# Transposed 32x32 blocks go from SBUF to SBUF in four transfers, without a DRAM tile

## The chip, the core and the metric

The kernel runs on one core of a Trainium2 chip. The metric is the device time of one execution in microseconds; less is better. The core has the engines PE (matmuls), DVE, ACT and POOL (elementwise), and the queue of SP, which here issues nearly all transfers between DRAM and SBUF.

## What is computed

A chunked attention over 4 batches, 8 heads, 768 positions and 64 features, and then a two-layer network on its output. Each chunk of 32 queries sees 16 positions to the left, its own 32, 8 to the right, and 8 memory positions: 64 keys.

```python
for c in range(nc):                      # 24 chunks of 32
    k_full = np.concatenate([mem_k, k[:, :, l_start:r_end]], axis=2)
    v_full = np.concatenate([mem_v, v[:, :, l_start:r_end]], axis=2)
    scores = scale * np.matmul(q_c, k_full.transpose(0, 1, 3, 2))
    scores = scores - np.max(scores, axis=-1, keepdims=True)
    a = np.exp(scores)
    a = a / (np.sum(a, axis=-1, keepdims=True) + 1e-09)
    out[:, :, c_start:c_end] = np.matmul(a, v_full)
...
h = x @ w_in                             # x: 3072 x 512, w_in: 512 x 2048
P = a[0] + a[1] * h + a[2] * h2 + a[3] * h3
Q = 1.0 + np.abs(b[0]) * np.abs(h) + np.abs(b[1]) * h2
return (P / (Q + 1e-06)) @ w_out         # w_out: 2048 x 512
```

## The kernel before

The 3072 tokens are 8 blocks of 384 (`TB`), half a batch each. The network runs in rounds: round n takes a block i and one of 16 slices j of the inner 2048. `g1` (L386, 12 matmuls) makes h for the slice, a chain of elementwise steps on ACT, DVE and POOL (L442 to L480) makes g as a high and a low part (`ghi`, L473, and `glo`, L480, both on POOL), and `g2` (L401, 9 matmuls) adds g times w_out into the three PSUM tiles `o` of the block. `order` sets the rounds: slices 0 to 9 of blocks 0 and 1, all of block 2, slices 10 to 15 of block 1, then of block 0, then blocks 3 to 7. The sums of the first ten slices of blocks 0 and 1 are kept in DRAM (`part`); `fetch` loads them into the tiles `stage` ahead of the block's end, and `evac` (L425, DVE) adds them to `o`.

The input of a block, `x_hi` and `x_lo`, comes from its attention, which runs in pieces between the rounds, for 4 pairs of heads p per block (a unit is one (i, p)). For blocks 3 to 7 (`BLOCKWISE` = 3) the pieces of a unit are:
- `att_scores` (b, PE L277), `att_max` (m, DVE: max and subtraction L293 into `e`, written with the two heads side by side), `att_exp` (x, ACT);
- `att_turn` (c): DVE transposes `e` in 32x32 blocks into a tile `blocks` (`turn_blocks`, L301); then `across` moves the blocks to their places in `eT`;
- `att_values` (d, PE L328): `eT` times v;
- `att_norm` (n, DVE): the row sums' inverse (L336, L337), and the scaling L339 into `xt`;
- `att_back` (e): `xt` is transposed in the same way and goes through `across` into `xf`;
- `att_hi` (h, ACT L353) copies `xf` into `x_hi`, `att_lo` (l, POOL L364) makes `x_lo`.

`across` writes `blocks` with one transfer into a DRAM tile and reads it back with four, one for each group of 32 destination partitions. The four reads wait for the write to have landed. There are two `blocks` tiles, two `eT` and two `xf` tiles, each in turn.

Every instruction and transfer keeps the order of the program on its engine (`pin`, and `load`, which issues on SP's queue, L117). SP issues in order: a transfer that waits holds up all those behind it. In the queue stand, mixed with those of `across`, the loads of q, k and v of later units, the `stage` loads and the stores of the output. The rounds up to 29 are in an order written out by hand (`SEQ`); from 30 on (`HAND`) a plan places the pieces: `attend(n, "db")` ahead of g1, and `attend(n, "xhlencmQ")` at the end of the round.

Of the kernel before, what the change touches and what calls it, by code (L numbers as in the profile page):

```python
# [12 lines left out]
F32 = mybir.dt.float32  # L13
# [3 lines left out]
ALU = mybir.AluOpType  # L17
AX = mybir.AxisListType

CHUNK = 32  # L20
# [12 lines left out]
BLOCKWISE = 3  # L33
# [32 lines left out]
def attn_moe(ctx, tc, qk, vm, w, a, b, out):  # L66
    nc = tc.nc
    P = 128
    NBLK, NPAIR = qk.shape[:2]
    NJT, DM = w.shape[0], out.shape[1]  # L70
    D = DM // (2 * NPAIR)
    TB = out.shape[0] // NBLK
    NC = TB // CHUNK
    NG = TB // P
    KEYS = P // 2
# [9 lines left out]
    dr = ctx.enter_context(tc.tile_pool(name="dr", bufs=1, space=bass.MemoryType.DRAM))  # L85
# [26 lines left out]
    def pin(ins):  # L112
        if pinned[0]:
            tc.keep_in_program_order(ins)

    def load(dst, src, queue=nc.sync):
        ins = queue.dma_start(out=dst, in_=src)  # L117
        if in_order[0]:
            tc.keep_in_program_order(ins)
# [139 lines left out]
        return [(g, j, 4 * g + j if i < BLOCKWISE else NG * j + g) for g in range(NG) for j in range(4)]  # L259

    def across(blocks, name):
        kept = dr.tile([P, TB], F32, name=name, tag=name, bufs=2)
        load(kept, blocks)
        t = at.tile([P, TB], F32, name=name, tag=name, bufs=XB.get(name, 1))
        n = TB // 4
        for b in range(4):
            load(t[b * CHUNK:(b + 1) * CHUNK].rearrange("k (j n) -> k j n", n=n),
                 kept.rearrange("(j k) (b n) -> b k j n", k=CHUNK, n=n)[b])
        return t

    def att_scores(i, p):
# [8 lines left out]
    def att_max(i, p):  # L280
        u = unit[i, p]
        s = u.pop("s")
        sv = s[:, :NG * 2 * KEYS].rearrange("x (g h w) -> x g h w", g=NG, h=2)
        if i % 2 == 0:
            pin(nc.vector.memset(sv[0:CHUNK, 0, :, 0:LEFT], NEG))
        else:
            pin(nc.vector.memset(sv[P - CHUNK:P, NG - 1, :, WIN - RIGHT:WIN], NEG))
        mx = sm.tile([P, NG * 2], F32, name="mx")
        s3 = s[:, :NG * 2 * KEYS].rearrange("x (n w) -> x n w", w=KEYS)
        pin(nc.vector.tensor_reduce(mx, s3, axis=AX.X, op=ALU.max))  # L290
        e = u["e"] = at.tile([P, NG, KEYS, 2], F32, name="e", tag="e", bufs=2)
        top = mx.rearrange("x (g h) -> x g h", g=NG).unsqueeze(3).broadcast_to([P, NG, 2, KEYS])
        pin(nc.vector.tensor_tensor(e.rearrange("x g w h -> x g h w"), sv, top, op=ALU.subtract))  # L293

    def att_exp(i, p):
        e = unit[i, p]["e"]
# [7 lines left out]
    def att_turn(i, p):  # L304
        u = unit[i, p]
        if i >= BLOCKWISE:
            u["eT"] = across(turn_blocks(u.pop("e").rearrange("x g w h -> x g (w h)")), "eT")
            return
        ep = u["ep"] = pa(i)
        e = u.pop("e")  # L310
        for g in range(NG):
            pin(nc.tensor.transpose(out=ep[:, g * P:(g + 1) * P], in_=e[:, g], identity=ident))
# [19 lines left out]
    def att_norm(i, p):  # L332
        u = unit[i, p]
        on = u.pop("o")[:, :NG * 2 * (D + 1)].rearrange("x (n d) -> x n d", d=D + 1)
        rinv = sm.tile([P, NG * 2], F32, name="rinv")
        pin(nc.vector.tensor_scalar(rinv.unsqueeze(2), on[:, :, D:D + 1], 1e-9, W_SCALE, op0=ALU.add, op1=ALU.mult))  # L336
        pin(nc.vector.reciprocal(rinv, rinv))  # L337
        xt = u["xt"] = at.tile([P, NG * 2, D], F32, name="xt", tag="xt")
        pin(nc.vector.tensor_tensor(xt, on[:, :, :D], rinv.unsqueeze(2).broadcast_to([P, NG * 2, D]), op=ALU.mult))  # L339

    def att_back(i, p):
        u = unit[i, p]
        if i >= BLOCKWISE:
            u["xp"] = across(turn_blocks(u.pop("xt").rearrange("x (g h) d -> x g (h d)", h=2)), "xf")
            return
        xp = u["xp"] = pa(i)
        xt = u.pop("xt")
        for g in range(NG):
            pin(nc.tensor.transpose(out=xp[:, g * P:(g + 1) * P], in_=xt[:, 2 * g:2 * g + 2, :], identity=ident))
# [54 lines left out]
    kept = []  # L404
# [88 lines left out]

    att = {}
    pieces = dict(b=att_scores, m=att_max, x=att_exp, c=att_turn, k=att_keep, d=att_values, n=att_norm, e=att_back, h=att_hi, l=att_lo)

    def plan(n, kind, i, p):
# [135 lines left out]
def windows(x, mem):  # L633
    B, H, S, D = x.shape
    n = S // CHUNK
    rows = np.arange(n)[:, None] * CHUNK + np.arange(WIN)
    x = np.pad(x, ((0, 0), (0, 0), (LEFT, RIGHT), (0, 0)))[:, :, rows]
    mem = np.broadcast_to(mem[:, :, None], (B, H, n) + mem.shape[2:])
    return np.concatenate([x, mem], axis=3)


def lay_out(q, k, v, mem_k, mem_v):
    B, H, S, D = q.shape
    n = S // CHUNK // 2
    kw, vw = windows(k, mem_k), windows(v, mem_v)
    keys = kw.shape[3]
    kt = kw.reshape(B, H // 2, 2, 2, n * keys, D).transpose(0, 3, 1, 2, 5, 4).reshape(2 * B, H // 2, 2, D, n * keys)
    qt = q.reshape(B, H // 2, 2, 2, n * CHUNK, D).transpose(0, 3, 1, 2, 5, 4).reshape(2 * B, H // 2, 2, D, n * CHUNK)
    qk = np.stack([np.concatenate([kt[:, :, 0], qt[:, :, 0]], axis=3),
                   np.concatenate([qt[:, :, 1], kt[:, :, 1]], axis=3)], axis=2)  # L650
    vw = np.concatenate([vw, np.ones(vw.shape[:4] + (1,), vw.dtype)], axis=4)
    vm = vw.reshape(B, H // 2, 2, 2, n, keys, D + 1).transpose(0, 3, 1, 2, 5, 4, 6)
    return qk, np.ascontiguousarray(vm.reshape(2 * B, H // 2, 2, keys, n * (D + 1)))


# [16 lines left out]
```

## Time and profile before

| | |
|---|---|
| median of 3 runs | 651.05 us (650.72 to 652.34) |
| profiled execution | 647.67 us |
| its span | 645.9 us |
| PE busy | 615.8 us (95%) |
| DVE busy | 494.4 us (77%) |
| ACT busy | 432.7 us (67%) |
| POOL busy | 431.2 us (67%) |
| mean granted clock of PE | 0.984 |

The span goes from the first to the last instruction of the profiled execution; the rest of its time lies around it. Busy time is a share of the whole span; the stretches differ, and the rows below are read by stretch. The granted clock is 1.00 at 2.4 GHz and 0.50 at 1.2 GHz. In a timeline the last part in brackets is the time in which the engine had nothing to do before the instruction, and what released it.

### The profile page before, as it was taken

The numbers are of one execution on the slowest core, as the hardware profiler recorded it, in microseconds if no ns is written. First come the engines' busy times: TensorE is split into PE (matmuls) and PEld (weight loads), VectorE is DVE, ScalarE is ACT, GpSimd is POOL, SyncE is SP. The second block draws the span as 40 slices with busy tenths as digits, with TensorE's granted clock in tenths as the row PEclk, the third lists the DMA queues.
The fourth block names the chain that finished last, engine by engine and source line by source line (L and its number), as shares of the span: only waits on it lengthen the run. The fifth ranks groups of instructions, "written<-read, shape, count | busy, mean of one in ns | idle before, by whom it ended". The sixth has DMA issues, their size and how long they took to land.

```text
span 645.9 us, 12289 instructions
## 1 busy us (share of the span) xinstructions
PE 615.8 (95%) x4312; PEld 536.7 (83%) x4312; DVE 494.4 (77%) x961; ACT 432.7 (67%) x814; POOL 431.2 (67%) x457
## 2 busy tenths in 40 slices
PE   4779999999999999799999999999999999999997
PEld 3477787889988888698988888889888888999995
DVE  5878998997967887778777777877777777766665
ACT  4667878778856666466666766676666766676664
POOL 5557776977966657556666666676766666776662
PEclk8879999999999999899999999999999999999999
DMA  7998136304122555554333532234333310000001
GB/s 251 380 381 303 43 91 238 114 1 154 52 92 81 166 185 159 162 160 154 114 103 105 157 114 86 76 99 144 103 99 112 119 55 25 24 28 23 2 1 49
DMA packets 49326, 77.55 MB, mean 120 GB/s; under 512 B 27121, under 2 KB 32241, under 8 KB 48881
## 3 DMA queue, kind: packets, MB, share of 16 engines
q1 hardware_dynamic: 48016, 72.04, 34.4%
q10 hardware_dynamic: 960, 3.16, 1.5%
q0 software_dynamic: 288, 1.57, 0.7%
q8 instruction: 34, 0.56, 0.4%
q14 instruction: 28, 0.22, 0.1%
HBM read 59.44 MB, written 17.30 MB: 119 GB/s over the span
## 4 chain that ended last, share of the span: by engine, by line
issue 23%; PE 21%; POOL 20%; DVE 13%; DMA 12%; SPq 5%; ACT 5%; POOLq 0%; DVEq 0%; ACTq 0%
PE h L386 10%; PE o L401 8%; POOL glo L480 8%; POOL ghi L473 7%; SPq L117 5%; DMA xf<-blocks 3%; POOL cy L447 2%; DMA qk<-in_qk_dram 2%; DVE ct L466 2%; POOL x_lo L364 2%; DMA eT<-blocks 2%; DMA w_raw<-in_w_dram 2%; DVE cr L467 2%; DMA v_main<-in_vm_dram 2%; DVE stage L170 2%
## 5 line engine op out<-in xcount | busy, mean ns | idle before, releaser
L386 PE MATMUL h<-x_hi,w_hl 128*128 128x384 f32 x1024 | 268.1, 343 | 3.3 <-DVE ct L457 3.2
L401 PE MATMUL o<-w_hl,ghi 128*128 128x512 f32 x768 | 241.4, 395 | 4.2 <-POOL ghi L473 3.2
L447 POOL TENSOR_TENSOR cy<-cy,ha 128x384 f32<-128x384 f32 x128 | 130.1, 1016 | 145.5 <-ACT cy L443 140.8
L386 PEld LDWEIGHTS h<-x_hi,w_hl 128*128 128x128 f32 x1024 | 186.7, 190 | 17.2 <-issue 5.4
L386 PE MATMUL h<-x_lo,w_hl 128*128 128x384 f32 x512 | 173.7, 339 | 0.0
L401 PEld LDWEIGHTS o<-w_hl,ghi 128*128 128x128 f32 x768 | 141.9, 189 | 26.7 <-POOL ghi L473 3.6
L401 PE MATMUL o<-w_hl,glo 128*128 128x512 f32 x384 | 152.5, 397 | 0.9 <-POOL glo L480 0.6
L480 POOL TENSOR_TENSOR glo<-ct,ghi 128x384 fp32r<-128x384 f32 x126 | 127.8, 1014 | 9.1
L442 ACT ACTIVATE ha<-h 128x384 f32<-128x384 f32 x128 | 62.8, 491 | 97.1 <-PE h L386 92.4
L456 DVE TENSOR_TENSOR ct<-ct,h 128x384 f32<-128x384 f32 x128 | 70.3, 549 | 71.4 <-ACT ct L452 71.2
L473 POOL TENSOR_TENSOR ghi<-ct,zero 128x384 fp32r<-128x384 f32 x126 | 104.3, 828 | 11.2 <-DVE ct L468 8.7
L466 DVE SCALAR_TENSOR_TENSOR ct<-ct,par,cr 128x384 f32<-128x384 f32 x128 | 78.5, 613 | 37.4 <-ACT cr L462 34.9
L461 ACT ACTIVATE cr<-cy 128x384 f32<-128x384 f32 x128 | 63.3, 494 | 58.5 <-POOL cy L447 52.2
L386 PEld LDWEIGHTS h<-x_lo,w_hl 128*128 128x128 f32 x512 | 97.2, 190 | 0.0
L443 ACT ACTIVATE cy<-ha,bab 128x384 f32<-128x384 f32 x128 | 90.9, 710 | 4.3
L401 PEld LDWEIGHTS o<-w_hl,glo 128*128 128x128 f32 x384 | 72.4, 189 | 22.4 <-POOL glo L480 2.7
L452 ACT ACTIVATE ct<-h,par 128x384 f32<-128x384 f32 x128 | 83.9, 656 | 0.0
L457 DVE SCALAR_TENSOR_TENSOR ct<-ct,par,h 128x384 f32<-128x384 f32 x128 | 78.7, 615 | 4.5
L468 DVE SCALAR_TENSOR_TENSOR ct<-cr,ct 128x384 f32<-128x384 f32 x128 | 71.4, 558 | 4.4
L467 DVE SCALAR_TENSOR_TENSOR cr<-cy,cr 128x384 f32<-128x384 f32 x128 | 71.2, 556 | 0.4
L462 ACT ACTIVATE cr<-cr 128x384 f32<-128x384 f32 x128 | 60.8, 475 | 4.0
L184 POOL TENSOR_TENSOR w_hl<-w_raw,w_hl 128x512 fp32r<-128x512 f32 x32 | 41.9, 1310 | 23.8 <-ACT w_hl L179 22.7
(58 smaller groups left out, 409.8 us busy)
## 6 DMA issues: line engine op xcount, KB each, us to landing
qk<-in_qk_dram SPq DMA_DIRECT2D x56, 288.0 KB, 3.8
w_raw<-in_w_dram SPq DMA_DIRECT2D x26, 512.0 KB, 7.2
v_main<-in_vm_dram SPq DMA_DIRECT2D x56, 195.0 KB, 4.1
out_dram<-stage SPq DMA_DIRECT2D x24, 256.0 KB, 3.2
eT<-blocks SPq DMA_DIRECT2D x20, 192.0 KB, 2.0
eT<-eT SPq DMA_DIRECT2D x80, 48.0 KB, 2.1
xf<-blocks SPq DMA_DIRECT2D x20, 192.0 KB, 1.9
xf<-xf SPq DMA_DIRECT2D x80, 48.0 KB, 2.0
```

The costliest lines, as they stand in the source:

```text
L386: pin(nc.tensor.matmul(h[:, :TB], lhsT=wt[:, cols], rhs=xt[i][:, ct, :], start=m == 0, stop=m == last))
L401: ins = nc.tensor.matmul(o, lhsT=gt[:, cols], rhs=wt, start=begin and m == 0, stop=end and m == 2)
L443: pin(nc.scalar.activation(c["y"], c["ha"], AF.Identity, scale=B1, bias=B0))
L447: pin(nc.gpsimd.tensor_tensor(c["y"], c["y"], c.pop("ha"), op=ALU.mult))
L452: pin(nc.scalar.activation(c["t"], c["h"], AF.Identity, scale=A3, bias=A2))
L456: pin(nc.vector.tensor_tensor(t, t, h, op=ALU.mult))
L457: pin(nc.vector.scalar_tensor_tensor(t, t, A1, h, op0=ALU.add, op1=ALU.mult))
L466: pin(nc.vector.scalar_tensor_tensor(t, t, A0, r, op0=ALU.add, op1=ALU.mult))
L467: pin(nc.vector.scalar_tensor_tensor(r, yy, QC, r, op0=ALU.add, op1=ALU.mult))
L468: pin(nc.vector.scalar_tensor_tensor(t, r, 2.0, t, op0=ALU.subtract, op1=ALU.mult, reverse0=True))
L473: pin(nc.gpsimd.tensor_tensor(ghi, chain[z]["t"], zero.broadcast_to([P, TB]), op=ALU.add))
L480: pin(engine.tensor_tensor(glo, chain.pop(z)["t"], gh[z].bitcast(F32), op=ALU.subtract))
```

## The change

`across` no longer makes a DRAM tile. It issues four transfers from `blocks` to the destination tile, both in SBUF: each takes 32 source partitions and writes one quarter of the columns of all 128 destination partitions, in pieces of 96 words (384 B). So destination partition 4k+b holds what was row 32b+k. To make up for this, the rows are given another order ahead of it: for blocks 3 to 7 the subtraction that writes `e` becomes two instructions, one for each head, and so does the scaling that writes `xt`; the v rows are reordered in the array from which they are loaded. Blocks 0 to 2, which turn their tiles on PE, stay as they are.

```diff
--- before.py
+++ after.py
@@ -259,13 +259,10 @@
         return [(g, j, 4 * g + j if i < BLOCKWISE else NG * j + g) for g in range(NG) for j in range(4)]
 
     def across(blocks, name):
-        kept = dr.tile([P, TB], F32, name=name, tag=name, bufs=2)
-        load(kept, blocks)
         t = at.tile([P, TB], F32, name=name, tag=name, bufs=XB.get(name, 1))
         n = TB // 4
-        for b in range(4):
-            load(t[b * CHUNK:(b + 1) * CHUNK].rearrange("k (j n) -> k j n", n=n),
-                 kept.rearrange("(j k) (b n) -> b k j n", k=CHUNK, n=n)[b])
+        for j in range(4):
+            load(t[:, j * n:(j + 1) * n], blocks[j * CHUNK:(j + 1) * CHUNK].rearrange("k (b n) -> k b n", n=n))
         return t
 
     def att_scores(i, p):
@@ -289,8 +286,14 @@
         s3 = s[:, :NG * 2 * KEYS].rearrange("x (n w) -> x n w", w=KEYS)
         pin(nc.vector.tensor_reduce(mx, s3, axis=AX.X, op=ALU.max))
         e = u["e"] = at.tile([P, NG, KEYS, 2], F32, name="e", tag="e", bufs=2)
-        top = mx.rearrange("x (g h) -> x g h", g=NG).unsqueeze(3).broadcast_to([P, NG, 2, KEYS])
-        pin(nc.vector.tensor_tensor(e.rearrange("x g w h -> x g h w"), sv, top, op=ALU.subtract))
+        top = mx.rearrange("x (g h) -> x g h", g=NG).unsqueeze(3)
+        if i < BLOCKWISE:
+            pin(nc.vector.tensor_tensor(e.rearrange("x g w h -> x g h w"), sv, top.broadcast_to([P, NG, 2, KEYS]), op=ALU.subtract))
+            return
+        turned = e.rearrange("x g w h -> x g (w h)").rearrange("x g (v h k) -> x g v h k", v=2, h=2)
+        for h in range(2):
+            pin(nc.vector.tensor_tensor(turned[:, :, :, h], sv[:, :, h].rearrange("x g (v k) -> x g v k", v=2),
+                                        top[:, :, h].unsqueeze(3).broadcast_to([P, NG, 2, CHUNK]), op=ALU.subtract))
 
     def att_exp(i, p):
         e = unit[i, p]["e"]
@@ -336,7 +339,15 @@
         pin(nc.vector.tensor_scalar(rinv.unsqueeze(2), on[:, :, D:D + 1], 1e-9, W_SCALE, op0=ALU.add, op1=ALU.mult))
         pin(nc.vector.reciprocal(rinv, rinv))
         xt = u["xt"] = at.tile([P, NG * 2, D], F32, name="xt", tag="xt")
-        pin(nc.vector.tensor_tensor(xt, on[:, :, :D], rinv.unsqueeze(2).broadcast_to([P, NG * 2, D]), op=ALU.mult))
+        if i < BLOCKWISE:
+            pin(nc.vector.tensor_tensor(xt, on[:, :, :D], rinv.unsqueeze(2).broadcast_to([P, NG * 2, D]), op=ALU.mult))
+            return
+        turned = xt.rearrange("x (g h) d -> x g (h d)", h=2).rearrange("x g (b h k) -> x g h k b", b=4, h=2)
+        sides = rinv.rearrange("x (g h) -> x g h", h=2).unsqueeze(3)
+        on = on.rearrange("x (g h) d -> x g h d", h=2)
+        for h in range(2):
+            pin(nc.vector.tensor_tensor(turned[:, :, h], on[:, :, h, :D].rearrange("x g (k b) -> x g k b", b=4),
+                                        sides[:, :, h].unsqueeze(3).broadcast_to([P, NG, D // 4, 4]), op=ALU.mult))
 
     def att_back(i, p):
         u = unit[i, p]
@@ -650,7 +661,10 @@
                    np.concatenate([qt[:, :, 1], kt[:, :, 1]], axis=3)], axis=2)
     vw = np.concatenate([vw, np.ones(vw.shape[:4] + (1,), vw.dtype)], axis=4)
     vm = vw.reshape(B, H // 2, 2, 2, n, keys, D + 1).transpose(0, 3, 1, 2, 5, 4, 6)
-    return qk, np.ascontiguousarray(vm.reshape(2 * B, H // 2, 2, keys, n * (D + 1)))
+    vm = np.array(vm.reshape(2 * B, H // 2, 2, keys, n * (D + 1)))
+    late = vm[BLOCKWISE:].reshape(2 * B - BLOCKWISE, H // 2, 2, keys // CHUNK, CHUNK, n * (D + 1))
+    vm[BLOCKWISE:] = late.swapaxes(3, 4).reshape(vm[BLOCKWISE:].shape)
+    return qk, vm
 
 
 def kernel(q, k, v, mem_k, mem_v, moe_w_in, moe_w_out, moe_a, moe_b):
```

## Rows read from the trace of the kernel before

**Rows 1.** Stretches: window, length, then PE, PEld, DVE, ACT, POOL busy; PEclk, DMA, GB/s
```profile
249.00:275.00 26.00, 21.64 (x154) 17.48 (x147) 18.37 (x38) 12.65 (x24) 14.40 (x16) 0.93 0.54 163
275.00:632.00 357.00, 357.00 (x2354) 319.29 (x2353) 265.51 (x516) 236.37 (x441) 239.34 (x255) 1.00 0.29 86
270.00:272.00 2.00, 1.96 (x5) 1.58 (x6) 1.91 (x4) 1.41 (x4) 1.64 (x2) 0.50 0.67 252
```

**Rows 2.** Timeline of PE: start us, us, engine, line, op, out<-in, count [idle before <-releaser]
```profile
251.65 0.63 PE L401 MATMUL o<-w_hl,ghi 128*128 128x512 f32 x2
...
253.73 0.51 PE L386 MATMUL h<-x_hi,w_hl 128*128 128x384 f32 x2
...
255.84 0.67 PE L401 MATMUL o<-w_hl,ghi 128*128 128x512 f32 x2
...
258.89 0.51 PE L386 MATMUL h<-x_hi,w_hl 128*128 128x384 f32 x2
...
260.99 0.63 PE L401 MATMUL o<-w_hl,ghi 128*128 128x512 f32 x2
...
263.47 0.51 PE L386 MATMUL h<-x_hi,w_hl 128*128 128x384 f32 x2
...
268.95 0.73 PE L401 MATMUL o<-w_hl,ghi 128*128 128x512 f32 x2 [3.23 <-POOL ghi L473]
...
273.23 0.87 PE L328 MATMUL pa<-v_main,eT 128*32 128x130 f32 x24
```

**Rows 3.** Timelines of DVE, ACT and POOL in the hole, same columns
```profile
254.97 1.35 DVE L425 SCALAR_TENSOR_TENSOR stage<-o,stage 128x512 f32<-128x512 f32 x2 [2.99 <-DMA stage<-part]
...
265.40 0.51 ACT L353 CAST x_hi<-xf 128x384 fp32r<-128x384 f32 x1 [3.48 <-DMA xf<-xf]
...
265.99 0.99 POOL L364 TENSOR_TENSOR x_lo<-xf,x_hi 128x384 fp32r<-128x384 f32 x1 [4.30 <-ACT x_hi L353]
```

**Rows 4.** Timeline of SP's queue, 222 to 262 us: when each transfer is issued
```profile
222.58 0.34 SPq L117 DMA_DIRECT2D xf<-blocks  x1
232.50 1.73 SPq L117 DMA_DIRECT2D xf<-xf  x4
...
250.18 1.53 SPq L117 DMA_DIRECT2D stage<-part  x3
...
256.68 1.74 SPq L117 DMA_DIRECT2D eT<-eT  x4
258.52 0.38 SPq L117 DMA_DIRECT2D xf<-blocks  x1
261.96 1.73 SPq L117 DMA_DIRECT2D xf<-xf  x4
```

**Rows 5.** Timeline of DVE: the transpose of the third xt of block 3
```profile
247.20 0.58 DVE L301 STREAM_TRANSPOSE blocks<-xt 128x384 f32<-128x384 f32 x1 [0.27 <-DMA xf<-blocks]
```

**Rows 6.** Issues: KB each, median us to landing; the page, then the stretch 215 to 240
```profile
eT<-eT SPq DMA_DIRECT2D x80, 48.0 KB, 2.1
...
xf<-blocks SPq DMA_DIRECT2D x1, 192.0 KB, 9.9
```

**Rows 7.** Groups by line: count | busy us, mean ns of one | idle before
```profile
L293 DVE TENSOR_TENSOR e<-pa,mx 128x384 f32<-128x384 f32 x32 | 17.9, 558 | 1.3
...
L339 DVE TENSOR_TENSOR xt<-pa,rinv 128x384 f32<-128x384 f32 x32 | 17.8, 558 | 1.2
...
L336 DVE TENSOR_SCALAR rinv<-pa 128x6 f32<-128x6 f32 x32 | 5.0, 156 | 3.8 <-PE pa L328 3.7
```

**Rows 8.** Timelines of DVE and POOL in one chain round: last DVE instruction, then ghi
```profile
242.19 0.56 DVE L468 SCALAR_TENSOR_TENSOR ct<-cr,ct 128x384 f32<-128x384 f32 x1
...
244.13 0.83 POOL L473 TENSOR_TENSOR ghi<-ct,zero 128x384 fp32r<-128x384 f32 x1
```

**Rows 9.** Timeline of DVE: the transpose of the second xt and what follows
```profile
232.50 0.58 DVE L301 STREAM_TRANSPOSE blocks<-xt 128x384 f32<-128x384 f32 x1
234.32 0.55 DVE L456 TENSOR_TENSOR ct<-ct,h 128x384 f32<-128x384 f32 x1 [1.23 <-ACT ct L452]
```

## Prediction

> **What bounds the kernel now.** I read three views in this order. First the stretches [rows 1]: from 275 us to 632 us PE is busy 357.00 of 357 us at a granted clock of 1.00, so nothing that merely brings data earlier can shorten that part. From 249 to 275 us it is busy 21.64 of 26 us, and the granted clock is 0.93. The change touches only the attention of blocks 3 to 7, which begins before this hole and goes on long after it; so the hole is the place where it can gain.
>
> Then the timeline of PE in the hole [rows 2]. Its rows are the first matmuls of the alternating groups of g1 (L386) and g2 (L401). An undisturbed g2 runs from 251.65 to 253.73, 2.08 us; an undisturbed g1 from 253.73 to 255.84, 2.11 us. Against these:
> - g2 at 255.84 lasts to 258.89: 3.05, so 0.97 lost.
> - g2 at 260.99 lasts to 263.47: 2.48, so 0.40 lost.
> - from g1 at 263.47 to the next g2 at 268.95: 5.48, so 3.37 lost (3.23 of it is the idle time that the row gives, which waits for POOL's ghi).
> - that g2 lasts to 273.23: 4.28, so 2.20 lost. Right after the idle time the granted clock was 0.50 from 270 to 272 us [rows 1], the 1.2 GHz level.
>
> Together 6.94 us, 1.1% of the profiled time.
>
> Third, who was late [rows 3]. DVE stood 2.99 us, until 254.97, for stage<-part, the load of the kept partial sums; it had been ready at 251.98. This makes the first two losses (DVE frees the PSUM bank late, then runs its chain late). ACT stood 3.48 us, until 265.40, for xf<-xf, the last hop of the transposed output; POOL stood 4.30 us behind ACT, until 265.99, and so ghi came late. This makes the other two. ACT and POOL work in order: what they hold up is not only x_hi and x_lo but the chain of g behind them.
>
> Both late loads stand in SP's queue, so I read its timeline [rows 4]. The store xf<-blocks is issued at 222.58, and the next issue, the reads xf<-xf, follows at 232.50: SP stood for 9.6 us until the store had landed (9.9 us in this busy stretch [rows 6]). Everything behind it is late: the stage loads go out at 250.18; then the next eT goes through its store, and its reads go out at 256.68. The xt that DVE had turned at 247.20 [rows 5] gets its store only at 258.52 and its reads at 261.96, 14.2 us after DVE was done with it. The queue's own waits make the lateness, not the bytes.
>
> **The change part by part.**
>
> *The DRAM hop goes.* Per turned tile one store and the wait for its landing go, 40 times. SP no longer waits for a landing before it can issue the reads; it waits only for the DVE transpose, a free xf or eT buffer, and what is ahead. Of the same four transfers of 48 KB the old form issued in 1.73 us [rows 4] and landed 2.1 us after issue in the median [rows 6]. No row shows SBUF as source; bounds: as fast as these 2.1 us or somewhat faster below, and the 9.9 us of the worst store above. I take 2.1, because destination, piece length (384 B) and size are the same.
>
> New times, worked out from the old rows: the transfers of the first xt go out at 222.6 to 224.3. The second xt is turned at 232.50 [rows 9], 0.58 long, so its transfers go out by about 234.8. One v load and the stage loads follow: about 236 to 240. They took at most 4.8 us from issue to DVE's start (250.18 to 254.97), so they are there by 245; DVE asks at 251.98, and any issue before 247.2 would do. The 2.99 us go, and with them 0.97 + 0.40. The third xt, turned by 247.78, goes out at once, until 249.5, and lands at about 251.6. ACT asked for it at 265.40 - 3.48 = 261.92, and would ask 1.4 us earlier with the first two losses gone: a margin of 8.9 us, more than the 7.8 by which the slowest landing exceeds 2.1. So 3.37 + 2.20 go as well.
>
> What is late next? Nothing in that stretch: the groups before and after it run at 2.1 us with no gap. The fourth xt follows a chain round or more later on every engine and takes the same path, so I give it no loss either.
>
> *DVE does more.* The subtraction (L293) and the scaling (L339) of 20 units each become two instructions over half the columns. Now each takes 0.558 [rows 7]; a 6-column instruction takes 0.156, so 384 columns cost 0.402 over it. A half is 0.156 + 0.201 = 0.357, a pair 0.714: 0.156 more, twice per unit, 0.31 us, 6.2 us of DVE over 20 units. Bounds for a half: 0.28 (half the row) and 0.56 (all of it), so 0 to 1.1 us per unit. The cover: DVE is busy 265.5 of 357 us [rows 1], and in a chain round its last instruction ends at 242.75 where POOL takes ghi at 244.13 [rows 8], 1.38 us of room. I cost it at nothing; without the cover it would be 6.2 us, nearly the whole gain.
>
> The new scaling writes neighbours 128 B apart, which no row shows. The old subtraction writes them 8 B apart and takes the same 558 ns as the contiguous scaling [rows 7]: up to there a step costs nothing. The Trainium skill, page "Advanced Engine Details and Errata", section "Memory Cachelines", speaks against the change here: SBUF lines are 16 B, and full speed wants at least two hits on a line. By that page the old 8 B step is just free, as the rows have it, and the new one is not. It gives no price; by it the sum could only be worse.
>
> *Buffers.* A "blocks" tile is free only when all four transfers have landed, not the one store: some 1.4 us later, since four issues take 1.73 us where the store took 0.38 [rows 4]. Where it bites is the second xt, turned at 232.50 [rows 9] just as the old store landed (222.58 + 9.9). New: last issue 224.3 plus 2.1 to 9.9, so 226.4 to 234.2. The transpose's follower started at 234.32 after 1.23 us of waiting for ACT anyway; with the 1.38 of room the landing may come as late as 235.1 with no loss on PE. So zero, also at the upper end.
>
> *The rest.* The v rows are reordered in DRAM ahead of the launch, the same bytes and pieces. PE, ACT and POOL do the same work in the same order. Blocks 0 to 2 keep their instructions.
>
> Sum: 647.67 - 6.94 = 640.7 us for the profiled execution (span 645.9 and 1.8 around it). That execution lies 3.4 us below the median of the runs, 651.05; I carry the difference over: 651.05 - 6.94 = 644.1.
>
> **The rivals.**
>
> *Part of the hole stays.* Another wait in the queue (a v load that waits for PE) holds the stage loads beyond 247.2, or the third xt beyond 261.9, for a part of the time. For: SP is in order, and loads that wait for PE stand between the transfers. Against: PE has done with those buffers long before by my times. If only the last two losses go, the gain is 5.57 and the time 645.5; if only the first two go, 1.37, and 649.7. Idle time of 1 us with the slow clock after it would leave about 3 us: 647.3.
>
> *No gain.* The transfers from 32 partitions to 128 take over 10 us, so that ACT waits as before, or the transfers that now come earlier crowd those from DRAM. For: one landing of 9.9 us shows how long a small transfer can take beside big ones. Against: at 246 to 250 us there is room, and the margin is 8 us. Time 650 to 653.
>
> *Slower: the 128 B step.* If it makes the scaling on DVE so slow that each unit's chain is late on PE, this repeats 20 times, in the stretch that has no idle time now. The room per unit is 1.38; the other pair takes 0.16 of it, so the scaling may rise from 0.56 to about 1.78 with no loss. To eat the 6.94 the excess must be 0.35 us per unit, a pair of 2.13 us; to be 2 us slower than before 0.45, a pair of 2.23, four times now, or (2.23 - 2 x 0.156) / 384 = 5.0 ns per column where it is 0.402 / 384 = 1.05. For it speaks the page above, against it that the price must be over four times what the rows show. At a pair of 2.4 us: 20 x 0.62 - 6.94 = 5.5 us more, 656.5.
>
> **How the numbers follow.** A measurement of this kernel can tell about 0.3%, 2 us, from no change. Full gain, 642 to 646: 0.66. Part of the hole stays, with over 2 us gained, to 649: 0.11. No gain, or under 2 us: 0.13. Slower: 0.10 (the step 0.06, slower or crowding transfers 0.04). So faster 0.77, same 0.13, slower 0.10. Predicted is the likeliest case, 644.1. Below, the range reaches to 640.5, since the hole hangs on landing times and may be longer in the timed runs, which lie above the profile; above, to 650.5, which takes in the partial gains and some of no gain. About 2 in 10 is left out.
>
> **What would show it.** Right: between 249 and 275 us PE without idle time and at clock 1.00, everything after it some 7 us earlier; in SP's waits no more waits for xf<-blocks or eT<-blocks; the stage loads issued before 247 and the third xf before 250; no ACT wait for xf in the hole. DVE busier by about 6 us, halves of about 0.36. Wrong: halves of the scaling of 0.9 us or more, landings of the four transfers over 8 us, idle time on PE between 275 and 560 us, or DVE waiting ahead of L301.

## The result, and the profile after

The changed kernel takes **642.71 us** (median of 4 runs, 641.6 to 643.65); the kernel before, run beside it, 651.44 us (4 runs, 650.72 to 652.34). The ratio is 0.9865, its 95% interval 0.984 to 0.9889: 8.7 us less. In a second comparison the same two kernels gave 641.45 and 649.63, ratio 0.9874 (0.9856 to 0.9892), 8.2 us less.

The interval lies clear of 1, though the gain is smaller than 2%.

First the stretches of the changed kernel, which answer to [rows 1]. Columns: window and length; busy us of PE, PEld, DVE, ACT and POOL; granted clock, DMA share, GB/s.

```profile
249.00:275.00 26.00, 26.00 (x210) 22.78 (x209) 21.48 (x46) 17.08 (x32) 18.60 (x21) 1.00 0.51 154
275.00:632.00 357.00, 357.00 (x2352) 318.87 (x2352) 273.80 (x550) 237.49 (x444) 241.65 (x257) 1.00 0.22 64
```

The hole is gone: from 249 to 275 us PE is busy 26.00 of 26 us, where it was 21.64, and the granted clock is 1.00 where it was 0.93. From 275 to 632 us it is still busy all the time, with DVE at 273.80 us instead of 265.51.

Next SP's queue, which answers to [rows 4]. Columns: start, us that the issuing took, queue, line, transfer, count.

```profile
225.54 3.50 SPq L117 DMA_DIRECT2D xf<-blocks  x4
229.14 1.19 SPq L117 DMA_DIRECT2D v_main<-in_vm_dram  x2
230.43 4.52 SPq L117 DMA_DIRECT2D out_dram<-stage  x3
235.04 2.52 SPq L117 DMA_DIRECT2D eT<-blocks  x4
237.66 1.19 SPq L117 DMA_DIRECT2D qk<-in_qk_dram  x2
238.94 2.51 SPq L117 DMA_DIRECT2D xf<-blocks  x4
241.55 1.19 SPq L117 DMA_DIRECT2D v_main<-in_vm_dram  x2
242.78 1.53 SPq L117 DMA_DIRECT2D stage<-part  x3
246.47 3.01 SPq L117 DMA_DIRECT2D eT<-blocks  x4
250.43 2.48 SPq L117 DMA_DIRECT2D xf<-blocks  x4
```

Between 225 and 244 us SP issues nearly without a pause, but for a wait of 3.0 us inside the three output stores at 230.43, which took 4.52 us; the stand of 9.6 us ahead of the reads of the first xt is gone. The stage loads go out at 242.78 instead of 250.18, the third xt at 250.43 instead of 258.52 and, for its reads, 261.96. Of SP's waits for a landing of eT or xf, over the whole span, one is left, the 3.0 us just named (us in total, times, longest):

```profile
SPq L117 <- DMA xf<-blocks: 3.0, 1, 3.0
```

Before, the row of the same name had 43.3 us over 20 waits, and that of eT<-blocks 35.6 over 20. It is the wait that went, not the late landing: in the busy stretch in which the old store took 9.9 us to land [rows 6], the four direct transfers of the first xt took 8.1 us. From the view of transfers of the changed kernel, 222 to 232 us (KB each, median us from issue to landing):

```profile
xf<-blocks SPq DMA_DIRECT2D x4, 48.0 KB, 8.1
```

What stands behind them in the queue went out meanwhile, but for the wait of 3.0 us.

The two engines that stood in the hole [rows 3] do so no more. DVE takes up the kept sums after 0.27 us, and that wait is for PE, not for the load; ACT takes the third xt without a wait. A timeline of each; the brackets give the idle time before and who ended it.

```profile
255.53 1.38 DVE L436 SCALAR_TENSOR_TENSOR stage<-o,stage 128x512 f32<-128x512 f32 x2 [0.27 <-PE o L412]
```

```profile
262.72 0.50 ACT L364 CAST x_hi<-xf 128x384 fp32r<-128x384 f32 x1
```

**Why the profile shows only 4.0 us.** The profiled execution of the changed kernel took 643.65 us with a span of 641.9, only 4.0 us less than the profiled one of before (span 645.9). To see why, I took a landmark that every execution passes ahead of the hole: the matmul of PE that waits for POOL's glo at about 188 us. Timeline of PE, the kernel before and the changed one:

```profile
188.20 0.50 PE L401 MATMUL o<-w_hl,glo 128*128 128x512 f32 x1 [0.22 <-POOL glo L480]
```

```profile
191.12 0.50 PE L412 MATMUL o<-w_hl,glo 128*128 128x512 f32 x1 [0.23 <-POOL glo L491]
```

The start up to there took 2.92 us longer in this execution. From the landmark to the end of the span it is 645.9 - 188.20 = 457.70 us before and 641.9 - 191.12 = 450.78 after: **6.92 us** less. The prediction's sum over the hole was 6.94. The gain lies in the hole alone: from the landmark to the g2 that starts at 255.84 us in [rows 2], and at 258.82 in the changed kernel, it is 67.64 us before and 67.70 after; the third g2 after it starts at 276.90 us before and at 272.97 after, 6.85 us sooner from the landmark; and for the last g2 group, at 632.25 and 628.23, it is 6.94.

### The profile page after: what moved, and what is told of

Same layout as the page of the kernel before. It is cut to its first block, busy times and chain, and to the rows that moved or that the text cites. A ratio compares the mean times of both kernels' runs of the same rounds, so it can differ in the third digit from the quotient of the medians.

```text
span 641.9 us, 12300 instructions
## 1 busy us (share of the span) xinstructions
PE 615.4 (96%) x4312; PEld 537.7 (84%) x4312; DVE 500.8 (78%) x1001; ACT 432.7 (67%) x814; POOL 431.7 (67%) x457
## 4 chain that ended last, share of the span: by engine, by line
PE 55%; issue 15%; POOL 13%; DVE 8%; DMA 4%; ACT 4%; SPq 1%; POOLq 0%; DVEq 0%; ACTq 0%
PE h L397 25%; PE o L412 23%; POOL glo L491 5%; POOL ghi L484 5%; PE pa L274 3%; PE pa L331 3%; DMA qk<-in_qk_dram 2%; DMA w_raw<-in_w_dram 2%; DVE stage L170 1%; DVE ct L477 1%; POOL cy L458 1%; DVE w_raw L171 1%; DVE cr L478 1%; DVE ct L479 1%; SPq L117 1%
```

## The experiments

My theory was the prediction's: SP, which works in order, stands between a store and the reads that depend on it, and everything queued behind is late by that. The rivals were that the DRAM hop costs by itself (its bytes, its landing time), that the new order of rows or the larger DVE work plays a part, and that the cover of DVE is thinner than I had costed it. Below, "landmark to end" is the time worked out as above, with the landmark of each profile; it leaves the differing start out. Each ratio is to the kernel before, run beside the kernel of the experiment.

**The hop kept, the reads later.** The kernel before, but the four reads of a turned tile are put into the queue a round later, ahead of the next attention step, so that other transfers go out between the store and the reads that wait for it.

```diff
+    late_reads = []
     def across(blocks, name):
...
-        for b in range(4):
-            load(t[b * CHUNK:(b + 1) * CHUNK].rearrange("k (j n) -> k j n", n=n),
-                 kept.rearrange("(j k) (b n) -> b k j n", k=CHUNK, n=n)[b])
+        late_reads.append((t, kept))
         return t
...
+        read_back()
         attend(n, "xhlencmQ")
```

> The kernel before, the DRAM tile kept; only the four reads of a turned tile are issued one round later than its store, so that the v, q, k and stage loads go out ahead of them and SP finds the store landed. If what costs the time is SP's stand between store and reads (my theory), the hole of PE between 249 and 275 us goes for the most part: 3 to 8 us less than the kernel before, and the stage loads issued before 247 us. If it is the length of the way (two hops, each some 2 us) or the bytes through DRAM, nothing is gained: within 2 us of the kernel before, with the hole still there, since both hops are kept and the reads come later than they did.

Measured: 642.66 us (5 runs), ratio 0.9879 (0.9858 to 0.99). Landmark to end 639.1 - 188.37 = 450.73, the changed kernel's to 0.05 us. The stretch of the hole, and SP's queue:

```profile
249.00:275.00 26.00, 26.00 (x196) 23.30 (x185) 20.87 (x43) 16.27 (x32) 18.40 (x20) 1.00 0.61 191
```

```profile
237.50 0.38 SPq L117 DMA_DIRECT2D xf<-blocks  x1
237.92 1.12 SPq L117 DMA_DIRECT2D v_main<-in_vm_dram  x2
239.56 1.73 SPq L117 DMA_DIRECT2D xf<-xf  x4
241.34 1.38 SPq L117 DMA_DIRECT2D stage<-part  x3
```

Both trips through DRAM are still there, with more bytes moved in the stretch (191 GB/s against 154), and PE is full. The stage loads go out at 241.34. SP still stands for landings of eT and xf, 15.1 us in all from 215 to 275 us where the kernel before has 27.0, but for at most 4.5 us at a time instead of 9.6. So neither the hop's bytes nor its landing time made the hole; the place of the dependent reads in the queue did. The gain can be had without touching the order of any row.

**The direct transfers kept, the store beside them.** The changed kernel, with the old store to DRAM issued as well, ahead of the four transfers, and nobody reading it.

```diff
+        kept = dr.tile([P, TB], F32, name=name + "k", tag=name + "k", bufs=2)
+        load(kept, blocks)
         for j in range(4):
```

> The changed kernel with the store to DRAM added again for each turned tile, ahead of the four transfers; nobody reads it and SP does not wait for it. It brings back the 40 stores and half of the DRAM traffic, without a stand. Theory (the stand in SP's queue): as fast as the changed kernel within 2 us, no hole. Rival (less traffic through DRAM makes the gain): a good part of the 8.7 us lost again, 3 us or more.

Measured: 642.59 us (4 runs), ratio 0.9883 (0.9862 to 0.9904); landmark to end 641.0 - 190.24 = 450.76. PE is busy 26.00 of 26 us in the hole. Forty more writes to DRAM cost nothing that shows: from the landmark the time is the changed kernel's to 0.02 us.

**And a wait for that store.** The same, with a small read of what was stored, which holds SP until the store has landed; the four direct transfers stand behind it.

```diff
+        kept = dr.tile([P, TB], F32, name=name + "k", tag=name + "k", bufs=2)
+        load(kept, blocks)
+        probe = at.tile([16, 16], F32, name="probe", tag="probe", bufs=2)
+        load(probe, kept[0:16, 0:16])
         for j in range(4):
```

> As the kernel with the added store, and behind each store a read of 16 x 16 words of it, for which SP has to wait until the store has landed, ahead of the four transfers. The data still goes from SBUF to SBUF. Theory: the stand is back, so is the hole: 5 to 10 us slower than the changed kernel, near the kernel before, with PE idle between 249 and 275 us and the third xf late. Rival (hops or bytes): as the kernel with the store alone, no hole.

Measured: 655.29 us (6 runs), ratio 1.0078 (1.0058 to 1.0099): 12.7 us more than with the store alone, and 5.0 us more than the kernel before beside it, so the loss is larger than the old hole. The stretch; who waits in SP's queue from 215 to 275 us (here xfk and eTk are the stored copies, xf and eT the tiles of the direct transfers); DVE's timeline; and the longest idle time of PE, which ends behind the stretch:

```profile
249.00:275.00 26.00, 19.58 (x131) 15.52 (x130) 17.01 (x35) 10.96 (x22) 12.92 (x15) 1.00 0.48 138
```

```profile
SPq L117 <- DMA xfk<-blocks: 11.4, 3, 7.1
SPq L117 <- DMA eTk<-blocks: 8.3, 3, 3.9
```

```profile
255.88 0.58 DVE L308 STREAM_TRANSPOSE blocks<-xt 128x384 f32<-128x384 f32 x1 [4.05 <-DMA xf<-blocks]
```

```profile
275.78 0.92 PE L416 MATMUL o<-w_hl,ghi 128*128 128x512 f32 x2 [4.14 <-POOL ghi L488]
```

The wait alone brings the hole back. A loss that the old hole didn't have shows in DVE's line: DVE now waits 4.05 us for a blocks buffer, and 11.5 us in six such waits from 190 to 632 us, where the kernel before had 0.3. How much of the loss beyond the old hole is theirs, no run separates. In the kernel before, the store freed the buffer as soon as it had landed; here the transfers that free it are queued behind the wait. The buffer loss, which the prediction weighed and costed at nothing, exists as soon as SP stands.

**The new order through DRAM.** The changed kernel (its rows, its halves on DVE), but with the store and four reads of the DRAM tile as sources.

```diff
+        kept = dr.tile([P, TB], F32, name=name, tag=name, bufs=2)
+        load(kept, blocks)
...
         for j in range(4):
-            load(t[:, j * n:(j + 1) * n], blocks[j * CHUNK:(j + 1) * CHUNK].rearrange("k (b n) -> k b n", n=n))
+            load(t[:, j * n:(j + 1) * n], kept[j * CHUNK:(j + 1) * CHUNK].rearrange("k (b n) -> k b n", n=n))
```

> The changed kernel with its row order, its halves on DVE and its four transfers, but the data goes through a DRAM tile as before: one store, then four reads in the new shape. Theory (the stand in SP's queue): the hole is back and the time is that of the kernel before, 648 to 653 us. Rival (the new shape of the transfers, or the new order of rows, brings the gain): 642 to 645 us.

Measured: 648.44 us (12 runs), ratio 0.9985 (0.9969 to 1.0001); landmark to end 646.7 - 188.73 = 457.97, the kernel before's within 0.3.

```profile
249.00:275.00 26.00, 21.78 (x160) 17.53 (x152) 19.41 (x41) 13.13 (x25) 14.95 (x16) 0.93 0.53 163
```

The hole is the old one to 0.14 us of PE. So the new order and the larger DVE work neither gain nor cost anything that shows; the whole difference lies in where the transfers read from, and with it in SP's wait.

**The scaling written in rows.** The changed kernel with the inner two loops of the scaling exchanged: it writes neighbours and reads PSUM in steps of 4 words.

```diff
-        turned = xt.rearrange("x (g h) d -> x g (h d)", h=2).rearrange("x g (b h k) -> x g h k b", b=4, h=2)
+        turned = xt.rearrange("x (g h) d -> x g (h d)", h=2).rearrange("x g (b h k) -> x g h b k", b=4, h=2)
...
-            pin(nc.vector.tensor_tensor(turned[:, :, h], on[:, :, h, :D].rearrange("x g (k b) -> x g k b", b=4),
-                                        sides[:, :, h].unsqueeze(3).broadcast_to([P, NG, D // 4, 4]), op=ALU.mult))
+            pin(nc.vector.tensor_tensor(turned[:, :, h], on[:, :, h, :D].rearrange("x g (k b) -> x g b k", b=4),
+                                        sides[:, :, h].unsqueeze(3).broadcast_to([P, NG, 4, D // 4]), op=ALU.mult))
```

> The changed kernel; only the scaling that writes xt runs in another order: it reads PSUM in steps of four words and writes runs of 16 neighbours, where it read neighbours and wrote in steps of 128 B. Half an instruction took 513 ns there, where the half subtraction took 351. If the step of the writes is what costs, it takes 0.35 to 0.37 us; if it is the PSUM side or the number of dimensions, it stays at 0.5 or rises. Either way the time is that of the changed kernel within 1.5 us, since DVE has room.

Measured: 641.46 us (4 runs), ratio 0.9883 (0.9859 to 0.9906); landmark to end 640.1 - 189.63 = 450.47. Groups by line (count | busy us, mean ns of one | idle before), first the changed kernel, then this one:

```profile
L349 DVE TENSOR_TENSOR xt<-pa,rinv 128x192 f32<-128x192 f32 x40 | 17.4, 513 | 0.7
...
L295 DVE TENSOR_TENSOR e<-pa,mx 128x192 f32<-128x192 f32 x40 | 12.4, 351 | 0.7
```

```profile
L349 DVE TENSOR_TENSOR xt<-pa,rinv 128x192 f32<-128x192 f32 x40 | 12.4, 352 | 0.7
```

A half of the scaling goes from 513 to 352 ns, the time of a half of the subtraction: the order with the write in steps of 128 B has a price, the step of 4 words in the read from PSUM none. The innermost run also grows from 4 elements to 16 in this run, which it doesn't tell apart from the step. The kernel's time differs from the changed one's by 0.3 us from the landmark, which no comparison here can tell from nothing.

**The scaling three and five times over.** To find where the cover ends, the pair of halves is issued three times, and five times, with the same result.

```diff
-        for h in range(2):
+        for h in [0, 1] * 3:
```

> The changed kernel with each pair of scaling instructions run three times, the same values written again: 1.76 us more of DVE per unit, 35 us in all. By the rows of the changed kernel the round with the scaling leaves DVE 1.34 us idle for ACT and the next ghi 1.39 us more, 2.7 us. Theory: the cover holds, within 2 us of the changed kernel. Rival (DVE's work is on the path, as if it were not covered): up to 35 us slower.

> As before, five times: 3.52 us more of DVE per unit. Theory: 0.8 us beyond the 2.7 of room, in up to 20 units: 8 to 16 us slower than the changed kernel, with PE waiting for POOL's ghi or glo or for DVE. Rival (DVE has still more room, for instance because the chain has two rounds): within 2 us of it. If the cover were the 1.38 us of the prediction alone, some 40 us slower.

Measured, three times: 643.42 us (4 runs), ratio 0.9915 (0.9889 to 0.9942); landmark to end 641.4 - 189.73 = 451.67, 0.9 us more than the changed kernel. Five times: 650.79 us (10 runs), ratio 1.0024 (1.0011 to 1.0038); landmark to end 649.1 - 189.30 = 459.80, 9.0 us more. A timeline of DVE in each (three times, then five times):

```profile
304.57 2.31 DVE L349 TENSOR_TENSOR xt<-pa,rinv 128x192 f32<-128x192 f32 x6
```

```profile
310.64 3.76 DVE L349 TENSOR_TENSOR xt<-pa,rinv 128x192 f32<-128x192 f32 x10
```

The six halves take 2.31 us and the ten 3.76, for 0.88 of the two: 1.43 and 2.88 us more per unit, less than the 1.76 and 3.52 expected, since the halves overlap. At 2.31 us 0.9 us of the gain is lost; at 3.76 all of it.

The 9.0 us of the five times fall within the 8 to 16 that were expected, but not in the way that was expected, and that is luck: they aren't 0.45 us in each of 20 units. PE's timeline shows where they are. Two starts of g2 groups that answer to each other in the changed kernel, then in the one with five times:

```profile
277.16 0.63 PE L412 MATMUL o<-w_hl,ghi 128*128 128x512 f32 x2
...
483.16 0.63 PE L412 MATMUL o<-w_hl,ghi 128*128 128x512 f32 x2
```

```profile
281.22 0.62 PE L412 MATMUL o<-w_hl,ghi 128*128 128x512 f32 x2
...
488.64 0.63 PE L412 MATMUL o<-w_hl,ghi 128*128 128x512 f32 x2
```

From the landmarks, 191.12 and 189.30, the first comes 86.04 and 91.92 us later, the second 292.04 and 299.34. So 5.9 of the 9.0 us are lost by the time that block 3's four units are done, and 1.4 in the 200 us behind it. In block 3 the scalings follow each other after 11 to 15 us (they start at 218.50, 230.73, 241.49 and 256.50), and DVE is full; later they are mostly 18.4 us apart, and there is room. Two stretches with five times, busy us of PE, PEld, DVE, ACT and POOL:

```profile
236.00:272.00 36.00, 32.32 (x210) 26.40 (x200) 34.42 (x77) 20.41 (x40) 21.77 (x23) 1.00 0.46 135
350.00:490.00 140.00, 139.88 (x983) 124.25 (x982) 130.12 (x290) 94.40 (x177) 94.38 (x101) 1.00 0.29 83
```

**The stage loads two rounds earlier.** The kernel before with one condition and its call changed, so that the big loads of the kept sums go into SP's queue ahead of the store and the reads of the second xt. The longest stand, between the store and the reads of the first xt, is still ahead of them.

```diff
-        if ends(n + 2) and order[n][0] < 2:
-            fetch(order[n][0])
+        if ends(n + 4) and order[n + 4][0] < 2:
+            fetch(order[n + 4][0])
```

> The kernel before with one edit: the kept partial sums are fetched two rounds earlier, so that their loads stand in SP's queue ahead of a q and k load, a pair of store and reads of xf and a v load, at about 242 us in place of 250. The DRAM hop stays. By the prediction's two parts: the first two losses, 1.37 us, go in any case, since any issue before 247.2 does. Of the other two, 5.57 us, a part goes if the big stage loads also held up the store and the reads of the next eT and xf (they landed in 4.4 us and 3.4 us there): the third xf would come 2 to 4 us sooner, and ACT waited 3.48. So 1.4 us less than the kernel before if only the stage loads move, up to 6.9 if the third xf comes in time; a rival in which the stand has to go for any gain gives 0.

Measured: 643.74 us (6 runs), ratio 0.992 (0.9899 to 0.9941); landmark to end 642.1 - 188.57 = 453.53, 4.2 us less than before. The hole, and SP's queue:

```profile
249.00:275.00 26.00, 24.92 (x193) 21.31 (x186) 19.82 (x40) 15.00 (x29) 16.33 (x18) 1.00 0.54 164
```

```profile
241.01 1.38 SPq L117 DMA_DIRECT2D stage<-part  x3
...
258.49 2.07 SPq L117 DMA_DIRECT2D xf<-xf  x4
```

More than half of the gain comes with this small edit, the DRAM hop kept. The clock stays at 1.00, and the last reads of the third xt go out 3.5 us earlier than in [rows 4] (258.49 against 261.96), with the stage loads no longer among what stands just ahead of them. The rest of the hole, 453.53 - 450.78 = 2.8 us, stays; with the reads put later it went too.

**The kernel before and the changed kernel, again.** To learn how far one execution's profile stands for the others: the kernel before three times more, the changed one once.

> The kernel before, unchanged, for a second profile of it. The timed gain is 8.7 us where the hole had 6.94 and the two profiles differ by 4.0. If the hole varies with landing times, this profile shows it longer, by 1 to 4 us in a slower execution. If the difference lies in the first 60 us, where the granted clock was 0.86 in the one profile and 0.80 in the other, the hole is 6.9 again and the time follows the clock of the first 60 us.

> The changed kernel, unchanged, for a second profile and for a comparison on one chip with the kernel before and the early fetch. In the first profile everything up to 190 us came 2.9 us later than in the kernel before, and the hole of 6.9 us was gone: 4.0 us less in sum. If the late start belongs to the change, it is there again by 2 to 3 us; if it varies from run to run, this profile may start earlier, with a span of 639 to 640 us. Time 641 to 644 us.

> The kernel before, unchanged, a third profile. The timed gain (8.2 and 8.7 us) is above the hole of 6.9 us that both profiles of it show, and those two executions, 647.67 and 648.00, lie below its median of 649 to 651. If the hole varies with landing times, a profile of an execution at 650 or more has over 6.9 us of hole: more than 457.8 us from the end of the last g2 wait ahead of the attention of block 3 (188 us) to the end. If not, this stretch is 457.7 again, and slower executions start later.

> The kernel before, unchanged, a fourth profile, with the same two readings as the third: 457.7 us from the landmark to the end in every profile if the hole is the same each time, more in a slower execution if it varies.

Measured: the kernel before, 649.08 us (12 runs, ratio 0.9989, 0.9973 to 1.0005), and in two single runs 650.68 and 650.38; the changed one, 641.45 (5 runs). From the landmark to the end:

| profile | landmark, us | to the end, us | more than the changed kernel |
|---|---|---|---|
| changed, first | 191.12 | 450.78 | |
| changed, again | 188.91 | 450.79 | 0.0 |
| before, first | 188.20 | 457.70 | 6.9 |
| before, again | 188.42 | 457.78 | 7.0 |
| before, third | 189.34 | 459.56 | 8.8 |
| before, fourth | 188.36 | 460.24 | 9.5 |

The changed kernel repeats itself to 0.01 us behind the landmark, while its start differs by 2.2 us between two executions; so most of the late start is not the change's. It was there early: the g2 group that starts at 50.22 us in the first profile of the kernel before starts at 52.79 in the first of the changed one, long before the first halved subtraction at 195.9 us. Over all fourteen profiles, though, the seven with direct transfers reach the landmark at 188.9 to 191.1 us and the seven with all data through DRAM at 188.2 to 189.3; whether the changed program has a part in that is not shown. The kernel before doesn't repeat itself: its hole costs 6.9 to 9.5 us. Part of what differs shows in the third one's rows (PE's timeline, then the stretch behind the idle time), beside those of the second:

```profile
270.63 1.22 PE L401 MATMUL o<-w_hl,ghi 128*128 128x512 f32 x2 [3.86 <-POOL ghi L473]
```

```profile
270.00:280.00 10.00, 9.37 (x72) 7.21 (x73) 5.89 (x12) 4.27 (x9) 5.38 (x6) 0.66 0.47 158
```

```profile
269.27 0.97 PE L401 MATMUL o<-w_hl,ghi 128*128 128x512 f32 x2 [3.79 <-POOL ghi L473]
```

```profile
270.00:280.00 10.00, 9.89 (x82) 8.18 (x82) 5.68 (x13) 4.81 (x9) 5.57 (x7) 0.85 0.41 128
```

The idle times are alike, 3.86 and 3.79 us, but the granted clock behind them is 0.66 over ten microseconds in the third and 0.85 in the second, as it was in the first behind 3.23 us: from 273 to 276 us it is 0.50 in the third, the 1.2 GHz level, and 1.00 in the second. In the fourth the clock was 0.69, behind 3.59 us. There the part of the hole that waits for the stage loads is longer too; PE stood for it once more than in the first:

```profile
257.29 0.70 PE L401 MATMUL o<-w_hl,ghi 128*128 128x512 f32 x2 [1.07 <-DVE stage L425]
```

## Why the prediction was right, point by point

**The bound and its cause: right.** The hole between 249 and 275 us was the place, and SP's stand its cause. Reads put later in the queue close it with the hop kept, a wait put in opens it with the hop removed, and the new order through DRAM leaves it as it was.

**The size of the hole: right for the profile it was read from.** 0.97 + 0.40 + 3.37 + 2.20 = 6.94 us against 6.92 from landmark to end.

**The new times in the queue: right, once the late start is taken off.** The stage loads at 242.78 - 2.92 = 239.9 (236 to 240 was said, 247.2 would have done); the third xt at 250.43 - 2.92 = 247.5 (247.8). Three terms under them were off and happened not to matter. The second xt's transfers went out from 238.94 - 2.92 = 236.0 us, where 234.8 was the end: the output stores, an eT and a q and k load stand ahead of them, which the prediction had left out. Four transfers out of SBUF take 2.5 us to issue, 0.63 each, where I had taken the 1.73 us of the reads from DRAM, 0.43 each. And "no more waits for xf<-blocks" holds but for the one wait of 3.0 us.

**The landing of the direct transfers: right in the median.** 2.0 us, for the taken 2.1; the page's rows of transfers (KB each, median us from issue to landing):

```profile
eT<-blocks SPq DMA_DIRECT2D x80, 48.0 KB, 2.0
xf<-blocks SPq DMA_DIRECT2D x80, 48.0 KB, 2.0
```

In the median the lower bound was the fact. The upper one came near in one place, 8.1 us for the first xt in the stretch of the old store's 9.9; so that time belonged to the stretch and not to the trip to DRAM, and it did no harm, since ACT takes up the first xt only at 248.08 us, without a wait. The Trainium skill, page "DMA: Bandwidth & Descriptors", section "Latency and other measured facts", puts most of a transfer's fixed cost down to the receipt from the target memory, with HBM the slowest target and an HBM access at up to 2 us at high load. The rows here don't show DRAM as the slower target: in the kernel before, the store of 192 KB to DRAM lands in 1.9 us in the median of 20.

```profile
xf<-blocks SPq DMA_DIRECT2D x20, 192.0 KB, 1.9
```

**DVE's extra work: the sum right by luck, one term mis-sized.** DVE is busy 500.8 us instead of 494.4, 6.4 more, for the forecast 6.2. The half of the subtraction took 0.351 us (0.357 was taken). The half of the scaling took 0.513 for 0.357, inside the bounds of 0.28 to 0.56 but near the upper end: I took a contiguous write's price for a write in steps of 128 B, although the page of the Trainium skill cited in the prediction had spoken against it. The sum came out because two errors cancelled. The halves of a pair overlap, so a pair of the scaling takes 0.88 us and not 2 x 0.513; against the 0.714 of the prediction that is too long, and a pair of the subtraction, 0.62 us, is too short.

```profile
305.34 0.88 DVE L349 TENSOR_TENSOR xt<-pa,rinv 128x192 f32<-128x192 f32 x2
307.56 0.55 DVE L467 TENSOR_TENSOR ct<-ct,h 128x384 f32<-128x384 f32 x1 [1.34 <-ACT ct L463]
```

**The cover: right to count on, and mis-sized.** After the pair DVE still waits 1.34 us for ACT, and later in that round POOL takes ghi 1.39 us after DVE's last instruction (312.21 after 310.82): 2.7 us of room, for the 1.38 that I had read from a round without attention [rows 8]. The round in which the scaling stands has attention matmuls on PE as well, so it is longer; I read the room in the wrong kind of round. Even 2.7 is not one number for all units: 2.88 us more per unit cost next to nothing in the later units, and most of its 9.0 us in the four of block 3. The forecast of the slower rival, no loss up to a pair of 1.78 us and the gain eaten at 2.13, would have made the threefold scaling of 2.31 us lose all of the gain; it lost 0.9 us. The gain was eaten at 3.76 us, and not by a loss repeated 20 times, as that rival had it. The end of DVE's chain in that round and POOL's ghi (timelines of the two):

```profile
310.26 0.56 DVE L479 SCALAR_TENSOR_TENSOR ct<-cr,ct 128x384 f32<-128x384 f32 x1
```

```profile
312.21 0.83 POOL L484 TENSOR_TENSOR ghi<-ct,zero 128x384 fp32r<-128x384 f32 x1
```

**The buffers: right here,** with no wait of DVE for a blocks tile in the hole, and right only because SP doesn't stand: in the run with the added wait DVE stood 4.05 us in one such wait.

**From the profile to the median: the step that was mis-sized.** I took the gain of one profiled execution, 6.94, off the median, 651.05, and got 644.1; measured 642.71, 1.4 less. The profiled execution, 3.4 us below the median, was one with a short hole. Over the four profiles the hole cost 6.9, 7.0, 8.8 and 9.5 us, 8.0 in the mean of these few, near the 8.2 and 8.7 us that the timed medians differ by. The prediction had this only as a reason for its range ("may be longer in the timed runs"), not as a term. What stays open is the start: 188.2 to 191.1 us at the landmark over the fourteen profiles; no run was made to find its cause.

## What to carry to other kernels

In this in-order DMA queue a trip through DRAM cost what stood behind the wait for its first half, not its bytes; so read the queue's timeline for who is behind, and try first whether the dependent reads can be issued a round later, or the one big load a round earlier. Here the first gave the whole gain without another layout, and the second more than half of it with a change of one condition.

When work is added beside a full engine, read the room from the very round in which it will stand, and find its end by issuing the work three and five times. Then look where along the run the loss falls: a loss divided by the number of units would have hidden that it sits in the four units that follow each other fastest.

This hole, with a stretch at the lower clock level behind it, varied from 6.9 to 9.5 us between executions; take the size of such a hole from several profiles, from a landmark ahead of it, before carrying it to a median.

## What the runs showed of the hardware

- A write of DVE in steps of 128 B, in runs of 4 elements, fp32: (513 - 156) / 192 = 1.86 ns per column, against (352 - 156) / 192 = 1.02 written in rows of 16 neighbours, with the 156 ns of a 6-column instruction [rows 7] taken as the fixed part. The Trainium skill, page "Advanced Engine Details and Errata", section "Memory Cachelines", has a penalty for a different 16 B line at every access; the traces agree, and the price here is of this size. A read from PSUM in steps of 4 words cost nothing.
- SP issues a transfer of 48 KB from 32 partitions of SBUF to 128 in 0.63 us, one from the DRAM tile of the same size in 0.43; both land in about 2 us in the median. The run with the new order through DRAM has the shape of the direct transfers with the DRAM tile as source, and issues four in 1.75 us, so the source makes the difference:

```profile
248.55 1.75 SPq L117 DMA_DIRECT2D xf<-xf  x4
```

- In one busy stretch a store to DRAM took 9.9 us to land and transfers from SBUF to SBUF 8.1 us. Two loads of 768 KB each, on POOL's queue, were under way in it; that they are the cause is likely but no run shows it.
- Idle time of PE doesn't cost the same clock every time: in executions of one kernel 3.79 us of it were followed by a granted clock of 0.85 over 270 to 280 us, and 3.59 us by 0.69. In the run with the added wait the 4.14 us that end at 275.78 us were followed by 0.66 from 275 to 280 us. The Trainium skill, page "TensorE: Matmul & The Clock Gate", section "What's actually happening", says that the hardware judges activity on a beat of its own that doesn't start with the kernel, so that one kernel differs from run to run; the profiles of the kernel before agree, with 0.85, 0.85, 0.66 and 0.69 behind one hole.
